# Reordering the first loads, casts and filler matmuls of a fused sigmoid-attention and MLP kernel on one core

## The chip, the core and the metric

The kernel runs on one core of a Trainium2 chip. The metric is device time in microseconds (us). Every run named here computed the right result. A profile is one execution; its span is some 1.8 us shorter than the time counted for that execution (388.1 against 389.91 us in the profile of before).

## The reference, cut to what matters

```python
# q, k, v: (8 batches, 12 heads, 448 rows, 64)
scores = scale * np.matmul(q, k.transpose(0, 1, 3, 2)) - np.log(S)
attn = 1.0 / (1.0 + np.exp(-scores))           # a sigmoid, no row sum
x = np.matmul(attn, v)                          # then reshaped to (3584, 768)
h = x @ w_in                                    # 768 -> 2048
g = 0.5 * h * (1.0 + np.tanh(c * (h + 0.044715 * h ** 3)))
out = g @ w_out                                 # 2048 -> 768
```

The kernel handles the heads in 24 groups of four. A group has seven column strips (`NJ`); one strip of one group is a unit: one score product on TensorE and one sigmoid of 128x896 values on ScalarE.

## The kernel before: the parts that the change touches

The kernel contains a planner. It plays the program forward with assumed costs and fixes the order of the instructions of each engine and of each queue. These orders are written into the program, so constants in the planner (assumed costs) act only through the order that they lead to.

k and q of group 0 arrive in two parts each, so that the first transposes can begin early. The later groups come in one transfer each.

```python
CUTS = ((0, NJ // 2 + 1), (NJ // 2 + 1, NJ))        # strips 0-3 and 4-6, for k and q
...
if g == 0:
    for x, (lo, hi) in enumerate(CUTS):
        # SyncE's queue: k.0, one half of q.1, k.1.   ScalarE's queue: q.0, the other half of q.1
        both = [plan.add(Op("ld%s0.%d.%d" % (nm, x, c), eng, ...))
                for (eng, c, w) in ((("SP", 0, 1), ("AQ", 1, 1)) if (nm, x) == ("q", 1) else
                                    (("AQ" if nm == "q" else "SP", 0, 2),))]
...
ld[g] = plan.add(Op("ld%s%d" % (nm, g), "AQ" if (nm, g) == ("q", 1) else "SP", ...))
...
who = "ACT" if (nm, x) == ("q", 0) else "DVE"       # which engine casts a part of group 0
```

Here k.0 is the first part of k, q.1 the second part of q, and k1 and q1 are k and q of group 1. `SP` is SyncE's queue, `AQ` ScalarE's, `DVE` is VectorE. A part that has landed is cast to bf16 (`qb`, `kb` in the profile), transposed on TensorE into `ps`, the program's PSUM tensor, and copied from there to `qT` or `kT`, which the score products read (a copy of 384 columns took 0.36 us on VectorE in the kernel before); then the scores of unit 0 can start.

Until there is real work, TensorE gets dummy matmuls. They are meant to have its clock granted in full by then. In the profile of before a matmul of 128 columns takes 107 ns at 5.1 us and 56 ns at 7.7 us; the turn is between 6.5 and 6.6 us, 5.0 us after the first dummy.

```python
def fn(e):
    return mm(ps[:, bank, 0:256], ident[:], gT[:, 0, 0:256], start=True, stop=True)
op = Op("warm", "PE", fn, [eye, blank, bank_free[bank]], 113.0 if plan.now > 6000.0 else 218.0, 165.0, mode=128)
...
if op is None and t < WARM and eye.end is not None and eye.end <= t and free_pairs(t) >= 2 and (...):
    return make_warm()
```

One helper does all casts and copies, so in the profile they share a line: L355 on VectorE and L354 on ScalarE, told apart by their tiles. The other lines are L412 dummies, L557 transposes of groups 0 and 1, L603 scores, L614 sigmoids of the first 21 units, L651 value products, L738 and L783 the two products of the MLP. In the changed kernel they are three to four lines further down, L358 and L357, L416, L560, L606, L617, L654, L741 and L786; some experiments move them a little more.

## Time and profile before

| | before |
|---|---|
| time, median of 3 runs (lowest to highest) | 390.36 us (390.03 to 390.97) |
| span of the profiled execution | 388.1 us |
| first sigmoid starts | 7.47 us |
| hole before the fifth sigmoid | 0.41 us |
| sixteenth sigmoid ends, and TensorE takes over as the bound | 21.06 us |

The page's busy times and two of its groups of instructions follow. In a group the columns are: line, engine, operation, output and input tiles, shapes, count, then busy time and mean ns of one, then the idle time of the engine just before them and what ended it.

```profile
PE 380.9 (98%) x3189; PEld 202.4 (52%) x3189; DVE 154.6 (40%) x268; ACT 228.2 (59%) x342; POOL 49.6 (13%) x82
...
L614 ACT ACTIVATE at<-ps 128x896 bf16<-128x896 f32 x21 | 17.2, 934 | 1.1 <-PE ps L603 1.1
...
L412 PE MATMUL ps<-gT,ident 128*128 128x256 bf16 x25 | 5.5, 380 | 1.5 <-POOL ident L362 1.5
```

TensorE is busy for 98% of the span, so there is little to win and it must be in the first 21 us. The 21 sigmoids of L614 were waited for 1.1 us in all: 0.66 before the first and 0.41 in the hole before the fifth. The dummies begin at 1.5 us, when GpSimd has made the identity.

### The profile page before, as it was taken

How to read it: one execution, taken by the hardware profiler on the slowest of the kernel's cores; microseconds unless marked ns; L12 is line 12 of the kernel's file. 1: busy time of each engine (PE TensorE's matmuls, PEld its weight loads, DVE VectorE, ACT ScalarE, POOL GpSimd, SP SyncE). 2: the span in 40 equal slices, each digit the busy share in tenths (PEclk: the TensorE clock that was granted, in tenths of full speed). 3: DMA queues.
4: the chain of work that ended last, by engine and by line, in shares of the span. 5: the costliest groups of instructions: out<-in, count | busy, mean ns of one | idle time of the engine just before them, and what ended most of it. 6: DMA issues, size and time to landing. Idle time of an engine off the chain costs nothing.

```text
span 388.1 us, 7458 instructions
## 1 busy us (share of the span) xinstructions
PE 380.9 (98%) x3189; PEld 202.4 (52%) x3189; DVE 154.6 (40%) x268; ACT 228.2 (59%) x342; POOL 49.6 (13%) x82
## 2 busy tenths in 40 slices
PE   7899999999999999999999999999999999999996
PEld 5434445545555555555555555555555555555565
DVE  3446633137760276404782068533571541000000
ACT  5999963258764575547684487655674772333221
POOL 5993110001200111001120011101000000000000
PEclk9999999999999999999999999999999999999999
DMA  8999999627791299804899247864472101111133
GB/s 228 195 203 203 210 207 311 138 64 183 188 225 26 59 208 196 200 2 120 184 243 197 47 109 175 219 121 95 113 195 53 42 2 41 43 41 42 41 83 81
DMA packets 64209, 51.74 MB, mean 133 GB/s; under 512 B 36272, under 2 KB 60720, under 8 KB 64176
## 3 DMA queue, kind: packets, MB, share of 16 engines
q1 hardware_dynamic: 48880, 36.77, 37.5%
q0 software_dynamic: 14528, 13.64, 23.1%
q10 hardware_dynamic: 768, 0.86, 0.7%
q8 instruction: 25, 0.41, 0.4%
q14 instruction: 8, 0.07, 0.0%
HBM read 45.61 MB, written 11.01 MB: 146 GB/s over the span
## 4 chain that ended last, share of the span: by engine, by line
PE 94%; ACT 3%; DMA 2%; DVE 0%; ACTq 0%; issue 0%
PE ps L783 38%; PE ps L738 37%; PE ps L603 9%; PE ps L651 8%; ACT at L614 3%; DMA qf<-in_q_dram 2%; PE ps L714 1%; PE ps L560 1%; ACTq L465 0%; DVE qb L355 0%; DVE kb L355 0%; PE ps L557 0%; ACT ob L354 0%
## 5 line engine op out<-in xcount | busy, mean ns | idle before, releaser
L623 ACT ACTIVATE th<-ps 128x896 f32<-128x896 f32 x147 | 127.5, 932 | 52.1 <-PE ps L603 52.1
L783 PE MATMUL ps<-w_out,gT 128*128 128x384 bf16 (+2 forms) x912 | 153.4, 323 | 0.0
L738 PE MATMUL ps<-xT,w_in 128*128 128x448 bf16 x750 | 148.0, 353 | 0.0
L783 PEld LDWEIGHTS ps<-w_out,gT 128*128 128x128 bf16 x912 | 86.9, 98 | 63.4 <-ACT th L623 3.7
L738 PEld LDWEIGHTS ps<-xT,w_in 128*128 128x128 bf16 x750 | 71.4, 98 | 71.9 <-issue 5.6
L627 DVE TENSOR_SCALAR at<-th 128x896 bf16<-128x896 f32 x147 | 91.7, 630 | 40.0 <-ACT th L623 39.0
L752 ACT ACTIVATE gT<-ps 128x448 bf16<-128x448 f32 x128 | 69.5, 554 | 63.7 <-PE ps L738 63.4
L355 DVE COPY ob<-ps 128x384 f32<-128x384 f32 x39 | 21.6, 554 | 75.1 <-PE ps L783 74.8
L603 PE MATMUL ps<-qT,kT 64*64 64x448 bf16 x672 | 48.1, 358 | 2.1 <-ACT at L614 1.7
L489 POOL DMA_DIRECT2D vb<-in_v_dram x24 | 15.0, 623 | 231.4 <-PE ps L603 228.3
L651 PE MATMUL ps<-at,vb 64*64 64x448 bf16 x672 | 38.2, 350 | 0.0
L603 PEld LDWEIGHTS ps<-qT,kT 64*64 64x64 bf16 x672 | 15.5, 105 | 26.5 <-issue 12.8
L354 ACT ACTIVATE ob<-ps 128x384 f32<-128x384 f32 (+2 forms) x18 | 8.5, 472 | 34.2 <-PE ps L783 34.2
L651 PEld LDWEIGHTS ps<-at,vb 64*64 64x64 bf16 x672 | 19.5, 107 | 12.2 <-issue 0.7
L355 DVE CAST kb<-kf 128x896 bf16<-128x896 f32 (+2 forms) x21 | 12.7, 606 | 27.6 <-DMA kf<-in_k_dram 27.6
L355 DVE CAST xT<-ps 128x448 bf16<-128x448 f32 x26 | 15.9, 622 | 11.1 <-PE ps L651 11.1
L614 ACT ACTIVATE at<-ps 128x896 bf16<-128x896 f32 x21 | 17.2, 934 | 1.1 <-PE ps L603 1.1
L355 DVE CAST qb<-qf 128x896 bf16<-128x896 f32 (+1 forms) x20 | 12.4, 618 | 10.7 <-DMA qf<-in_q_dram 10.5
L491 POOL DMA_DIRECT2D vb<-in_v_dram x24 | 15.8, 659 | 0.1
L354 ACT ACTIVATE xT<-ps 128x448 bf16<-128x448 f32 x22 | 12.2, 559 | 1.9 <-PE ps L651 1.9
L840 POOL DMA_DIRECT2D w_in<-in_moe_w_in_dram x16 | 9.9, 656 | 0.0
L412 PE MATMUL ps<-gT,ident 128*128 128x256 bf16 x25 | 5.5, 380 | 1.5 <-POOL ident L362 1.5
(30 smaller groups left out, 43.9 us busy)
## 6 DMA issues: line engine op xcount, KB each, us to landing
out_dram<-ob SPq DMA_DIRECT2D x54, 192.0 KB, 2.8
kf<-in_k_dram SPq DMA_DIRECT2D x19, 448.0 KB, 5.4
qf<-in_q_dram SPq DMA_DIRECT2D x18, 448.0 KB, 6.3
vb<-in_v_dram POOLq DMA_DIRECT2D x48, 112.0 KB, 5.7
w_in<-in_moe_w_in_dram POOLq DMA_DIRECT2D x16, 192.0 KB, 10.7
w_out<-in_moe_w_out_dram POOLq DMA_DIRECT2D x4, 768.0 KB, 21.9
kb<-in_k_dram POOLq DMA_DIRECT2D x4, 224.0 KB, 8.5
qb<-in_q_dram POOLq DMA_DIRECT2D x4, 224.0 KB, 9.0
```

Of the source, the lines that this page charges most:

```text
L354: return e.activation(o, i, AF.Copy)
L355: return e.tensor_copy(o, i)
L489: a = plan.add(Op("ldv%da" % g, "SWQ", lambda e, d=dst[0:64], ap=lo: e.dma_start(d, ap), deps, 610.0, 0.0, prio=order_v(g), sem="ldv%da" % ...
L491: c = plan.add(Op("ldv%db" % g, "SWQ", lambda e, d=dst[64:128], ap=hi: e.dma_start(d, ap), deps, 610.0, 0.0, prio=order_v(g), sem="ldv%db" ...
L603: r = mm(ps[64 * half:64 * half + 64, (x, y)[a], 0:S], kv[d, a, j, :], qv[d, a, :, :], start=True, stop=True)
L614: lambda e: e.activation(at[as_][:], both, AF.Sigmoid, bias=bias, scale=scale),
L623: lambda e: e.activation(th[ts][:], both, AF.Tanh, bias=0.5 * bias, scale=0.5 * scale),
L627: lambda e: e.tensor_scalar(at[as_][:], th[ts][:], 0.5, 0.5, op0=ALU.mult, op1=ALU.add),
L651: r = mm(ps[64 * c:64 * c + 64, banks[a], 0:S], vb[s][d, slot, j, :], at[as_][d, a, :], start=(j == 0), stop=(j == NJ - 1))
L738: r = mm(ps[:, bank, 0:S], w_in[:, kt, fc * 128:(fc + 1) * 128], xT[xb][:, kt, :], start=(kt == 0), stop=(kt == KT - 1))
L752: lambda e: e.activation(gT[:, fc, col:col + S], ps[:, bank, 0:S], AF.Gelu_apprx_tanh),
L783: r = mm(ps[:, bank, 0:hi - lo], gT[:, fc, col:col + 128], w_out[:, fc, lo:hi], start=(fc == 0), stop=(fc == FC - 1))
```

## The change

The intent is to start the sigmoids earlier and to close the hole before the fifth. k is cut into strips 3+4, so its first part is smaller. SyncE's queue carries k.0, all of q.1, then k1 and q1; ScalarE's carries q.0, then k.1. VectorE casts and copies q.0 and ScalarE q.1, the other way round than before. The dummies need only a blank tile and are 128 columns wide near the first real work, and none is put just ahead of it (`coming`). k1 now comes before q1.

```diff
-    DMA_FIRST = {"SP": 0.0, "AQ": 0.0, "SWQ": 1300.0}
+    DMA_FIRST = {"SP": 500.0, "AQ": 700.0, "SWQ": 1300.0}
...
+            w = 256 if plan.now < FINE else 128
-                return mm(ps[:, bank, 0:256], ident[:], gT[:, 0, 0:256], start=True, stop=True)
+                return mm(ps[:, bank, 0:w], gT[:, 0, 0:128], gT[:, 0, 0:w], start=True, stop=True)
...
-        CUTS = ((0, NJ // 2 + 1), (NJ // 2 + 1, NJ))
+        CUTS = {"q": ((0, NJ // 2 + 1), (NJ // 2 + 1, NJ)), "k": ((0, 3), (3, NJ))}
...
-                                for (eng, c, w) in ((("SP", 0, 1), ("AQ", 1, 1)) if (nm, x) == ("q", 1) else
-                                                    (("AQ" if nm == "q" else "SP", 0, 2),))]
+                                for (eng, c, w) in (("AQ" if (nm, x) in (("q", 0), ("k", 1)) else "SP", 0, 2),)]
...
-                ld[g] = plan.add(Op("ld%s%d" % (nm, g), "AQ" if (nm, g) == ("q", 1) else "SP",
+                ld[g] = plan.add(Op("ld%s%d" % (nm, g), "SP",
...
-                        who = "ACT" if (nm, x) == ("q", 0) else "DVE"
+                        who = "ACT" if (nm, x) == ("q", 1) else "DVE"
...
+        def coming(t):
+            wait = [cast.get(g if x is None else (g, x)) for (g, nm, src, dst, cast, tr, freed, after, x) in trans[:1]]
+            ends = [d.end for d in wait if d is not None]
+            ...
+            return any(e is not None and t < e <= t + NEAR for e in ends)
...
-            if op is None and t < WARM and eye.end is not None and eye.end <= t and free_pairs(t) >= 2 and (
+            if op is None and t < WARM and blank.end is not None and blank.end <= t and not coming(t) and free_pairs(t) >= 2 and (
```

The remaining lines of the diff are assumed costs. Only the first groups' instructions change their order; everything later stands in the same order on every engine.

More of the change, by code (lines that the diff above doesn't have):

```diff
@@ L319, in bass_sigmoid_attention__then__act_gelu_tanh_kernel @@
     WARM = 11000.0
+    FINE = 3400.0
+    FIRST = 44.0
+    NEAR = 50.0
     HOLD = 200.0
@@ L409, in make_warm @@
             bank = take(plan.now)
+            w = 256 if plan.now < FINE else 128
             def fn(e):
-                return mm(ps[:, bank, 0:256], ident[:], gT[:, 0, 0:256], start=True, stop=True)
-            op = Op("warm", "PE", fn, [eye, blank, bank_free[bank]], 113.0 if plan.now > 6000.0 else 218.0, 165.0, mode=128)
+                return mm(ps[:, bank, 0:w], gT[:, 0, 0:128], gT[:, 0, 0:w], start=True, stop=True)
+            op = Op("warm", "PE", fn, [blank, bank_free[bank]], w * (0.44 if plan.now > 6500.0 else 0.84), 165.0, mode=128)
             give(bank, op)
@@ L462, in load_qk @@
                 if g == 0:
-                    for x, (lo, hi) in enumerate(CUTS):
+                    for x, (lo, hi) in enumerate(CUTS[nm]):
                         both = [plan.add(Op("ld%s0.%d.%d" % (nm, x, c), eng,
@@ L467, in load_qk @@
                                             [], 490.0, 0.0, prio=(2, -3 if x == 0 else -2 if nm == "q" else -1),
-                                            sem="ld%s0.%d.%d" % (nm, x, c), pkt=(8 * w, 89.0 * (hi - lo) / NJ)))
-                                for (eng, c, w) in ((("SP", 0, 1), ("AQ", 1, 1)) if (nm, x) == ("q", 1) else
-                                                    (("AQ" if nm == "q" else "SP", 0, 2),))]
+                                            sem="ld%s0.%d.%d" % (nm, x, c), pkt=(8 * w, FIRST * (hi - lo) / NJ)))
+                                for (eng, c, w) in (("AQ" if (nm, x) in (("q", 0), ("k", 1)) else "SP", 0, 2),)]
                         ld[(0, x)] = All(both)
@@ L504, in cast_qk @@
                 if g == 0:
-                    for x, (lo, hi) in enumerate(CUTS):
-                        who = "ACT" if (nm, x) == ("q", 0) else "DVE"
+                    for x, (lo, hi) in enumerate(CUTS[nm]):
+                        who = "ACT" if (nm, x) == ("q", 1) else "DVE"
                         cast[(0, x)] = plan.add(Op("cast%s0.%d" % (nm, x), who,
@@ L509, in cast_qk @@
                                                        e, o[:, :, lo:hi, :], i[:, :, lo:hi, :], w),
-                                                   [ld[(0, x)]] + ([lambda: tr_q.get((0, 1))] if (nm, x) == ("k", 1) else []), (hi - lo) * 100.0, (hi - lo) * 110.0 + 150.0,
+                                                   [ld[(0, x)]] + ([lambda: tr_q.get((0, 1))] if (nm, x) == ("k", 1) else []), (hi - lo) * (107.0 if who == "ACT" else 75.0) + 60.0, (hi - lo) * (107.0 if who == "ACT" else 68.0) + 190.0,
                                                    prio=(0, -9 if nm == "q" or x == 0 else -1)))
@@ L548, in make_trans @@
             to = ps[:, bank, 0:NJ * 64].bitcast(BF16)
-            lo, hi = (0, NJ) if x is None else CUTS[x]
+            lo, hi = (0, NJ) if x is None else CUTS[nm][x]
             low = low_load(nm, g)
@@ L566, in make_trans @@
             flat_o = dst[:].rearrange("p j x -> p (j x)")[:, 128 * lo:128 * hi]
-            if (nm, x) == ("q", 0):
+            if (nm, x) == ("q", 1):
                 alts = {"ACT": ((hi - lo) * 107.0 + 50, (hi - lo) * 107.0 + 190)}
             else:
-                alts = {"DVE": ((hi - lo) * 70.0 + 70, (hi - lo) * 70.0 + 190)}
+                alts = {"DVE": ((hi - lo) * 70.0 + 70, (hi - lo) * 68.0 + 160)}
             tr[key] = plan.add(Op("trc%s%s" % (nm, key), "ANY",
@@ L582, in qk_needs @@
                 return [tr_q.get(g), tr_k.get(g)]
-            return [tr_q.get((0, 0)), tr_q.get((0, 1)), tr_k.get((0, 0 if j < CUTS[0][1] else 1))]
+            return [tr_q.get((0, 0)), tr_q.get((0, 1)), tr_k.get((0, 0 if j < CUTS["k"][0][1] else 1))]
         def by_half(t):
@@ L1025, in enter @@
             return n < 2 * UB or state["last"] == "b" or not go_b or state["av"] < NG * min(B, state["a"][0] + 1)
+        def coming(t):
+            wait = [cast.get(g if x is None else (g, x)) for (g, nm, src, dst, cast, tr, freed, after, x) in trans[:1]]
+            ends = [d.end for d in wait if d is not None]
+            if state["n"] < len(units):
+                needs = qk_needs(*units[state["n"]])
+                if all(d is not None and d.end is not None for d in needs):
+                    ends.append(max(d.end for d in needs))
+            return any(e is not None and t < e <= t + NEAR for e in ends)
         def pe_busy(pl, t):
             op = pe_next(pl, t)
-            if op is None and t < WARM and eye.end is not None and eye.end <= t and free_pairs(t) >= 2 and (
+            if op is None and t < WARM and blank.end is not None and blank.end <= t and not coming(t) and free_pairs(t) >= 2 and (
                     not state["n"] or sum(1 for x in range(state["n"]) if tanh[x].end is None or tanh[x].end > t) >= 2):
```

## The prediction

> **What bounds the kernel now.** I read the page's chain of work first, then busy time by stretch, then the timeline of the first 12 us, then the idle time by releaser.
>
> ```profile
> PE 94%; ACT 3%; DMA 2%; DVE 0%; ACTq 0%; issue 0%
> ```
>
> The chain that ended last is matmul work for 94% of 388.1 us. ScalarE and a transfer hold the other 5%. The table by stretch (columns: stretch, its length, then busy us of PE, weight load, VectorE, ScalarE, GpSimd, then granted clock, DMA share, GB/s) says where these lie:
>
> ```profile
> 1.50:5.10 3.60, 3.58 (x17) 2.54 (x18) 0.43 (x1) 1.86 (x3) 0.46 (x1) 1.00 0.86 274
> ...
> 7.04:11.20 4.16, 3.17 (x36) 1.47 (x37) 2.34 (x5) 3.34 (x4) 4.16 (x8) 1.00 1.19 189
> ...
> 19.00:21.10 2.10, 1.48 (x24) 0.37 (x16) 0.99 (x2) 2.10 (x4) 2.10 (x4) 1.00 1.24 201
> ...
> 61.00:200.00 139.00, 139.00 (x1132) 73.64 (x1130) 68.37 (x119) 81.79 (x118) 12.01 (x18) 1.00 0.65 150
> ```
>
> From 21.1 us TensorE is busy in every stretch without a hole, until the last matmul at 385. Before that it has holes, and ScalarE is full. So the kernel has three stages: a head until the first sigmoid, a sigmoid stage in which ScalarE paces everything, and a TensorE stage of fixed length. The diff touches only the head and the first group or two. Its whole worth is how much earlier the TensorE stage can begin, and that is how much earlier the sixteenth sigmoid ends (21.06 us). The chain in order of time names that stretch:
>
> ```profile
> 1.80 7.09 DMA qf<-in_q_dram
> 8.89 0.02 issue
> 8.91 0.73 DVE qb L355
> 9.64 0.60 DVE kb L355
> 10.25 0.05 issue
> 10.29 0.56 PE ps L557 x7
> 10.86 0.34 PE ps L603 x4
> 11.20 0.02 issue
> 11.22 9.84 ACT at L614 x12
> ```
>
> Columns are start, length, what. The binding thing is not the first sigmoid but the load of q for group 1: it lands at 8.89, VectorE casts q, then k; TensorE transposes k, and only behind those transposes stands the score product of unit 4 (a unit is one score tile pair and its sigmoid). ScalarE had run four sigmoids from 7.47 and then had nothing:
>
> ```profile
> 7.47 3.34 ACT L614 ACTIVATE at<-ps 128x896 bf16<-128x896 f32 x4 [0.66 <-PE ps L603]
> 11.22 2.54 ACT L614 ACTIVATE at<-ps 128x896 bf16<-128x896 f32 x3 [0.41 <-PE ps L603]
> ```
>
> The 0.41 in brackets is the hole. The starts within these runs are 0.80 to 0.82 us apart, the pace of ScalarE. So two terms can be won: the hole, and an earlier first sigmoid. They add, because all later sigmoids follow at the same pace.
>
> The head itself:
>
> ```profile
> 4.73 0.63 ACT L354 ACTIVATE qb<-qf 128x512 bf16<-128x512 f32 x1 [0.95 <-DMA qf<-in_q_dram]
> 5.12 0.63 PE L557 MATMUL ps<-ident,kb 128*128 128x128 bf16 x4
> 5.34 0.36 DVE L355 CAST qb<-qf 128x384 bf16<-128x384 f32 x1 [0.55 <-DMA qf<-in_q_dram]
> 5.54 0.95 PE L557 MATMUL ps<-ident,qb 128*128 128x128 bf16 x7
> 6.54 0.36 DVE L355 COPY qT<-ps 128x384 bf16<-128x384 bf16 x1 [0.32 <-PE ps L557]
> 7.04 0.57 PE L603 MATMUL ps<-qT,kT 64*64 64x448 bf16 x8
> ```
>
> The second part of q lands at 5.24 (the cast waits for it), is cast by 5.70, but its three transposes start only at 5.97: eleven stand in a row at 107 ns each, begun at 5.12 though k's cast was done at 4.79, because dummies (213 ns each) were still in front. Copy to 6.89, scores at 7.04, sigmoid at 7.47. Landing to sigmoid: 2.23 us.
>
> [...]both queues together reach 343 to 388 GB/s between 3.5 and 7 us[...]. [...]between 5 and 6 us I count 281 KB on ScalarE's queue against 51 on SyncE's. So who stands beside q's second part matters. [...]The trace shows 107 ns per 128-column transpose at 5.1 to 6.2 us and 56 ns at 7.7 us, the turn near 6.5, 5.0 us after the first dummy at 1.52.
>
> **The change part by part.**
>
> Transfers. Per DMA engine a descriptor takes 36 ns at 768 bytes (3 strips), 46 at 1024 (4), 74 at 1792 (all 7) in this trace, 16 of them per engine for a two-half transfer. Before, q's second part is complete after 16x46 (k's first) + 16x46 (q's first) + 2x8x36 = 2.05 us of engine time. After, if nothing else is served: 16x36 + 16x46 + 16x36 = 1.89 us, which is 0.16 earlier, landing 5.1. But k's second part now shares ScalarE's queue and can take turns with it[...]. I take 5.2, an estimate between them. k's first part gets smaller and should land 0.1 to 0.4 earlier than 4.34.
>
> Engines. ScalarE now casts and copies q's second part, 384 columns. From its rows for 512 columns (629 and 597 ns) and 0.85 ns a column, an estimate from the sigmoid's 934 ns at 896, the cast is 0.52 and the copy 0.49; VectorE took 0.36 for either. That costs 0.29. What it buys: k has three transposes instead of four, the dummies are 128 columns wide (107 ns) near the casts, and TensorE is kept free just ahead of a transpose, so q's last three need not queue. Sum from landing: 0.02 + 0.52 cast + 0.07 hand-over + 0.53 transposes (2x0.107 + 0.314, cold) + 0.04 + 0.49 copy + 0.08 + 0.43 scores to sigmoid = 2.18 us, so first sigmoid at 7.38 against 7.47: 0.09 won. VectorE's four-strip part (landing about 4.5, cast 0.43, four transposes, copy 0.42) ends about 6.0 and hides.
>
> Dummies. They no longer wait for the identity (1.52) but only for the blank tile (about 1.05). They are beside everything; they may bring the warm clock 0.45 earlier[...]. A warm clock would make the transposes 0.2 shorter.
>
> Group 1. k goes before q on SyncE's queue, both behind 384 KB. So k lands about 8, is cast and transposed by 9.5 at the latest, and unit 4 is needed at 7.38 + 4x0.81 = 10.62. The hole of 0.41 goes. Now q lands last, near 9.4 (same total bytes as before, when the last landed at 9.33). In the new TensorE order its transposes stand before unit 5: 9.4 + 0.75 cast + 0.06 + 0.39 + 0.19 (one value product) + 0.43 = 11.22 for unit 5's sigmoid, needed at 7.38 + 5x0.81 = 11.43. It hides, with 0.2 to spare. The instruction order of the other engines is unchanged after the first three groups.
>
> Sum: 0.41 + 0.09 = 0.50 us off 390.36, so 389.86; I say **389.85**. Weights follow: the first w_in slice landed at 22.77 and is used at 24.1, so half a microsecond fits.
>
> **The rivals.** First, q of group 1 becomes the wait: if it lands at 9.8, unit 5 starts at 11.62, against 12.04 before, and the gain is held to 0.4 whatever the head does: 389.95. For it: 0.2 of slack, GpSimd's loads start earlier since they wait for k's first part and take turns with q. Against: the total bytes are the same. Second, the second half of q lands at 5.4 behind k's second part and ScalarE's slower two steps stay: first sigmoid 7.6, the hole still gone, gain 0.3: 390.1. Third, the warm clock comes early and q lands at 5.1: first sigmoid 7.1, gain 0.75 (then the first rival caps it): 389.6. Fourth, the gap left ahead of the transposes delays the warm clock past 8 us: unit 0 and 1 at half pace, loss of 0.2 to 0.4: no gain at all.
>
> **Range and chances.** The rivals span 389.5 to 390.4. The three runs of before span 0.94 us, so the median carries some 0.3 of its own. Range 389.2 to 390.4. Two per cent is 7.8 us, and the whole head is 7.47, so faster than that is not to be had; nothing on the TensorE stage gets longer. Faster 0.01, within 2% 0.98, slower 0.01.
>
> **What would show each step.** First sigmoid at 7.1 to 7.6, q's second part landing at 5.1 to 5.4, ScalarE's cast 0.52 and copy 0.49. No idle before ScalarE's fifth sigmoid; sixteenth ending about 20.55; TensorE without a hole afterwards, last matmul about 384.5. The prediction is wrong if a hole opens before the sixth sigmoid (first rival), if TensorE waits for w_in near 23.5, or if the first sigmoid is earlier than 7.0 (transfers then served the small parts better than I worked out).

The forecast's sum is 0.41 + 0.09 = 0.50 us off 390.36, which gives 389.86 and was put as 389.85. Of the terms behind the 0.09, the working of the late end of q.1's landing, 5.4 us, is cut; the 5.2 used is the author's estimate between 5.1, worked out from the descriptor times of the trace of before (36 ns for 768 bytes, 46 for 1024), and that 5.4. The 0.45 us for an earlier full clock was an estimate too, from the starts of the dummies at 1.52 and about 1.05, and is not in the sum; measured, the matmuls turn to full pace between 6.5 and 6.6 us in both profiles (6.56 and 6.52 us in the record of the clock), though the dummies of the kernel after begin 0.43 us earlier.

## The result and the profile after

| | before | after |
|---|---|---|
| time, median (lowest to highest, runs) | 390.46 us (390.03 to 390.97, 4) | 389.75 us (389.67 to 390.08, 4) |
| span of the profiled execution | 388.1 us | 388.0 us |
| k.0 and q.0 landed | 4.34, 4.71 us | 4.21, 4.59 us |
| q.1 landed | 5.24 us | 5.45 us |
| k.1 landed | 7.19 us | 5.88 us |
| k1 and q1 landed | 9.33, 8.89 us | 7.16, 8.93 us |
| first sigmoid | 7.47 us | 7.57 us |
| hole before the fifth sigmoid | 0.41 us | none |
| sixteenth sigmoid ends | 21.06 us | 20.64 us |

The ratio of the two kernels is 0.9983 (95% interval 0.9966 to 1.0). Here and below a ratio is the mean time of one kernel's runs over the mean of the other's in the same rounds, so it is not quite the ratio of the quoted medians. The profiled executions took 389.91 and 389.75 us, so the two profiles have only 0.16 us between them to explain, less than the 0.7 us between the medians.

The page after, first the shares of the chain of work that ended last, then the sigmoids' and the dummies' groups:

```profile
PE 92%; ACT 4%; DMA 3%; issue 0%; DVE 0%; SPq 0%
...
L617 ACT ACTIVATE at<-ps 128x896 bf16<-128x896 f32 x21 | 17.1, 941 | 0.5 <-PE ps L606 0.5
...
L416 PE MATMUL ps<-gT 128*128 128x128 bf16 (+1 forms) x30 | 4.9, 329 | 1.6 <-DVE gT L408 1.1
```

The sigmoids' wait fell from 1.1 to 0.5 us, and 0.49 of that is the wait before the first. The dummies now begin after 1.1 us instead of 1.5, and there are 30 instead of 25. The transfers' share of the chain rose from 2% to 3%, which the last part of this section takes up.

The chain in order of time, from the load of q.1 on (start, length, what):

```profile
1.26 4.19 DMA qf<-in_q_dram
...
5.47 0.53 ACT qb L357
...
6.05 0.52 PE ps L560 x3
...
6.59 0.50 ACT qT L357
...
7.13 0.41 PE ps L606 x4
...
7.57 13.08 ACT at L617 x16
```

The chain now enters the sigmoid stage through the head, not through q1: q.1 lands at 5.45, is cast by ScalarE in 0.52 us, transposed, copied in 0.49 us, and sixteen sigmoids follow without a break. Group 1 stands in the timeline (start, busy time, engine, line, operation) like this:

```profile
8.98 0.63 DVE L358 CAST qb<-qf 128x896 bf16<-128x896 f32 x1
...
9.66 0.56 PE L560 MATMUL ps<-ident,kb 128*128 128x128 bf16 x7
...
10.16 0.38 PE L606 MATMUL ps<-qT,kT 64*64 64x448 bf16 x4
```

q1 is cast as soon as it has landed, and the score product of unit 4 begins at 10.16 us, before its sigmoid's turn. So the hole is closed.

Now the later stage. The kernel after is 0.41 us ahead at the sixteenth sigmoid, yet ends only 0.14 us ahead (its last matmul starts at 384.62 us, against 384.76). The chains show where the difference went. Before:

```profile
260.75 2.39 PE ps L738 x12
...
272.54 0.50 PE ps L603 x8
273.04 1.32 PE ps L651 x28
274.37 0.38 PE ps L603 x8
274.74 2.38 PE ps L738 x12
```

After:

```profile
260.34 2.39 PE ps L741 x12
...
267.11 5.94 DMA kf<-in_k_dram
...
273.08 0.06 DVE kb L358
...
273.62 0.56 DVE ob L358
...
274.23 0.38 PE ps L606 x4
274.61 2.38 PE ps L741 x12
```

At 260 us the lead is still 0.41 us (260.75 against 260.34). At 274.6 it is 0.13 us. In between TensorE waited for VectorE, as the timeline of the kernel after has it (the brackets hold the idle time and what ended it):

```profile
273.08 0.63 DVE L358 CAST kb<-kf 128x896 bf16<-128x896 f32 x1 [4.19 <-DMA kf<-in_k_dram]
...
273.62 0.55 DVE L358 COPY ob<-ps 128x384 f32<-128x384 f32 x1
...
274.23 0.11 PEld L606 LDWEIGHTS ps<-qT,kT 64*64 64x64 bf16 x4 [0.51 <-DVE ob L358]
```

VectorE stood still for 4.19 us in front of a cast whose load (k of group 22) had not landed. Behind that cast stood the copy of an output tile, which frees the PSUM banks that the next score product needs. That load took 5.94 us here and 5.61 in the profile of before, where the same cast ended early enough to leave no hole. So a stage that had no hole in one execution has one in another, and the orders of the instructions there are the same in both kernels.

### The profile page after: what moved, and what is told of

Its sections match the earlier page's. It is cut to its first block, busy times and chain, and to the rows that moved or that the text cites. A ratio compares the mean times of both kernels' runs of the same rounds, so it can differ in the third digit from the quotient of the medians.

```text
span 388.0 us, 7466 instructions
## 1 busy us (share of the span) xinstructions
PE 380.8 (98%) x3194; PEld 202.1 (52%) x3194; DVE 154.3 (40%) x268; ACT 228.1 (59%) x342; POOL 50.4 (13%) x82
## 4 chain that ended last, share of the span: by engine, by line
PE 92%; ACT 4%; DMA 3%; issue 0%; DVE 0%; SPq 0%
PE ps L786 38%; PE ps L741 37%; PE ps L606 9%; PE ps L654 7%; ACT at L617 3%; DMA kf<-in_k_dram 2%; DMA qf<-in_q_dram 1%; PE ps L717 1%; PE ps L563 1%; DVE ob L358 0%; ACT qb L357 0%; PE ps L560 0%; ACT qT L357 0%; SPq L469 0%; ACT ob L357 0%
## 5 line engine op out<-in xcount | busy, mean ns | idle before, releaser
L358 DVE CAST qb<-qf 128x896 bf16<-128x896 f32 (+1 forms) x20 | 12.3, 613 | 7.3 <-DMA qf<-in_q_dram 7.2
L416 PE MATMUL ps<-gT 128*128 128x128 bf16 (+1 forms) x30 | 4.9, 329 | 1.6 <-DVE gT L408 1.1
```

The source lines that it names most:

```text
L358: return e.tensor_copy(o, i)
```

## The experiments

Twelve runs were made, in four sets, each on one chip: the first four below; then the late casts, the swap and q1 on ScalarE's queue; then the nine dummies and the kernel before again; then the best version. The kernel before ran in the rounds of the first, third and fourth set. The second set, on the chip of the first, is held against the eleven runs of before of the first set and one more. "Hole" means idle time of ScalarE between two sigmoids, or of TensorE after 21 us. Landing times are those of the completion in the trace.

### The change again

No edit. The question is how large the effect is beside the spread between runs.

> The changed kernel unaltered, for its spread and a second profile. Every theory: ratio to the kernel before 0.998, as in the result (389.75 against 390.46 us). In the profile: first sigmoid near 7.57, sixteenth ending near 20.64. Open: whether the TensorE hole of 0.43 us at 273.8 us, seen in one profile, comes back (my theory: yes, within 0.2, because VectorE stands in front of a k load that takes 5.6 to 6 us).

Median 390.27 us (389.66 to 392.06, 6 runs), the kernel before 390.08 (389.46 to 390.94, 11 runs); ratio 1.0007 (0.9989 to 1.0026). The gain of the first measurement is not there. The head of this profile behaves like the first one's: first sigmoid 7.64, no hole, sixteenth ending at 20.71. But the late wait grew:

```profile
274.60 0.11 PEld L606 LDWEIGHTS ps<-qT,kT 64*64 64x64 bf16 x4 [0.81 <-DVE ob L358]
```

It is the same place as before, with 0.81 in place of 0.51, which is more than the 0.2 us that I had allowed. Two things therefore needed an explanation: this late hole, and the single run of 392.06 us.

### Only the order of group 1, on the kernel before

```diff
-ld[g] = plan.add(Op("ld%s%d" % (nm, g), "AQ" if (nm, g) == ("q", 1) else "SP",
+ld[g] = plan.add(Op("ld%s%d" % (nm, g), "SP",
```

q1 goes behind k1 on SyncE's queue. If the order k1, q1 is what closes the hole, this alone should close it. The edit does more than that, though: the planner answered it with another order on the engines. VectorE casts k1 first, and on TensorE the transposes of k1 and q1 each stand one unit earlier, those of q1 now in front of the fifth score product and not behind it.

> The kernel before with one edit: q of group 1 goes behind k of group 1 on SyncE's queue. Theory A (the gain is the hole before the fifth sigmoid, which the load of q for group 1 made): the hole of 0.41 us goes, first sigmoid stays at 7.47, sixteenth ends at 20.6, and the kernel is as fast as or 0.1 us faster than the changed one, ratio 0.998 to 0.9985. Theory B (the gain comes from the head: new strips, short dummies, earlier warm clock): no gain, ratio 0.9995 to 1.0005, and a hole stays.

The expectation missed. Median 391.15 us (390.88 to 391.35, 5 runs) against 390.08; ratio 1.0023 (1.0008 to 1.0038), so it is slower by 0.2%. The first sigmoid comes at 7.34, but:

```profile
9.59 0.38 PE L603 MATMUL ps<-qT,kT 64*64 64x448 bf16 x4
...
10.14 0.66 DVE L355 CAST qb<-qf 128x896 bf16<-128x896 f32 x1 [1.11 <-DMA qf<-in_q_dram]
...
10.85 0.56 PE L557 MATMUL ps<-ident,qb 128*128 128x128 bf16 x7 [0.89 <-DVE qb L355]
...
11.35 0.38 PE L603 MATMUL ps<-qT,kT 64*64 64x448 bf16 x4
...
11.79 1.73 ACT L614 ACTIVATE at<-ps 128x896 bf16<-128x896 f32 x2 [0.85 <-PE ps L603]
```

k1 landed at 8.38 and q1, issued at 2.74, only at 10.12. VectorE waited for it 1.11 us and ScalarE lost 0.85 us before the fifth sigmoid, whose score product (11.35) stands behind q1's transposes (10.85). This is the wait of the prediction's first rival, one unit earlier because of the moved order. With the order of before the same landing would still leave a hole of some 0.4 us before the sixth sigmoid (an estimate: the scores of 11.35 led to a sigmoid at 11.79, and the sixth is due at 7.34 + 5 x 0.81 = 11.39). The run is a loss, but how much of it is the loads' order and how much TensorE's is not separated; and of the 1.38 us by which its profile is longer than that of before, only 0.55 stand at the sixteenth sigmoid (21.61 against 21.06), the rest was lost later. In the full change something else must bring q1 in earlier.

### The change with k.1 on SyncE's queue

```diff
-for (eng, c, w) in (("AQ" if (nm, x) in (("q", 0), ("k", 1)) else "SP", 0, 2),)
+for (eng, c, w) in (("AQ" if (nm, x) == ("q", 0) else "SP", 0, 2),)
```

This takes k.1 away from the side of q.1. Between 4 and 5 us the kernel after moved 213 packets on SyncE's queue, where q.1 stands, and 212 on ScalarE's, where k.1 stands. If k.1 beside it is what delayed q.1 to 5.45, then q.1 should land earlier.

> The changed kernel with k's second part of group 0 moved from ScalarE's queue to SyncE's, behind q's second part; nothing else moves. Theory A (q's second part landed at 5.45 and not 5.1 because k's second part took turns with it on the other queue): it lands at 5.0 to 5.15, first sigmoid 7.2 to 7.3, sixteenth ends near 20.3, 0.3 us less than the changed kernel, unless a wait later takes it back. Rival: landing is set by the start of SyncE's queue or by its smaller descriptors, stays at 5.4, and nothing moves.

Half of it held. The engines' orders are those of the kernel after. q.1 landed at 5.22 and the first sigmoid came at 7.17, 0.40 earlier than in the kernel after. But q1, now issued fifth on the queue at 2.78, landed at 10.15:

```profile
12.22 0.92 ACT L617 ACTIVATE at<-ps 128x896 bf16<-128x896 f32 x1 [0.89 <-PE ps L606]
```

The hole of 0.89 us, before the sixth sigmoid, is the prediction's first rival as it was written. It took more than the head gave; the sixteenth sigmoid ended at 21.24. Median 390.81 us (389.62 to 392.04, 6 runs), ratio 1.0016 (0.9997 to 1.0034). Together with the run before it, this shows what the parts are for. k.1 on ScalarE's queue costs some 0.2 us of q.1's landing (5.45 against 5.22, one profile each), and it brings q1 from 10.15 to 8.93. Without it the new order of group 1 leaves a hole in both profiles. Why one more entry on SyncE's queue costs q1 over 1 us, when it is issued only 0.5 us later and the bytes are the same, was not settled. The traces show that q1's last packets come slowly beside GpSimd's loads between 8 and 10 us (21 packets of SyncE's queue in this run, 28 in the run before, 1 in the kernel after); that the packets of GpSimd's queue hold them up is argued, not shown.

### The change with one late cast moved

```diff
+    + ([lambda: ev_o.get((16, 0))] if (nm, g) == ("k", 22) else [])      # an added dependence of the cast
```

The cast of k for group 22 goes behind the copy of the output tile that stood behind it. If the copy behind the waiting cast makes the hole at 274 us, it goes.

> The changed kernel with one swap on VectorE, at 273 us: the copy of output strip 16's first half goes before the cast of k for group 22, which waits for its load. Theory A (the 0.27 us that the changed kernel loses between 273 and 280 us in its profile is the copy waiting behind that cast, and with it a PSUM bank): no TensorE hole over 0.33 us after 21 us, and 0.2 to 0.3 us less than the changed kernel, ratio near 0.9975. Rival (a fault of that one profile, or the delay moves to the next wait): same time as the changed kernel within 0.1 us.

The hole at 274 us is gone, and the median is 389.90 us (389.43 to 390.58, 6 runs), ratio 0.9993 (0.9979 to 1.0006). But the profiled execution, the longest of the six, has the same thing at another place:

```profile
202.35 0.63 DVE L358 CAST kb<-kf 128x896 bf16<-128x896 f32 x1 [1.90 <-DMA kf<-in_k_dram]
...
206.71 1.50 PE L742 MATMUL ps<-xT,w_in 128*128 128x448 bf16 x7 [0.83 <-DVE ob L358]
```

A cast waited 1.90 us for its load, VectorE ran late, and some 4 us further on TensorE waited for an output copy. So there are several such places, and which of them opens differs from one execution to the next.

### Four late casts moved, on both kernels

```diff
+    + ([lambda: ev_o.get((0, 0))] if (nm, g) == ("q", 6) else [])
+    + ([lambda: ev_o.get((16, 0))] if (nm, g) == ("k", 22) else [])
+    + ([lambda: ev_o.get((12, 0))] if (nm, g) == ("k", 17) else [])
+    + ([lambda: ev_o.get((12, 0))] if (nm, g) == ("q", 17) else [])
```

The same four dependences were added to the kernel before and to the changed one. With the late holes out of the way, the difference between the two should be the head's.

> The kernel before, with four casts on VectorE moved behind output copies so that no cast that waits for a load stands ahead of a copy that frees a PSUM bank (q of group 6 behind the first copy of strip 0, k and q of group 17 behind that of strip 12, k of group 22 behind that of strip 16). Theory C (the spread of all kernels, 389.4 to 392.1 us, is made by TensorE holes at 65, 206 and 274 us, whose length is that of a load's flight): no hole over 0.33 us after 22 us, spread of five runs below 0.5 us, median 0.1 to 0.5 us below the kernel before (its own profile had no such hole, its runs of 390.6 to 391 would). Rival D (the spread comes from elsewhere): spread and median as before.

> The changed kernel with the same four casts moved. Theories A and C: the head's 0.35 to 0.45 us, lost or hidden in the holes until now, shows in the time: 0.4 us below f1_before_late, about 389.4 us, spread below 0.5 us. Rival: the gain of the head is taken back wherever TensorE meets a transfer that does not come earlier with it; then f2_after_late equals f1_before_late within 0.1 us.

Before with late casts: median 389.76 us (389.61 to 390.3), ratio 0.9993 (0.9979 to 1.0007). After with late casts: median 389.60 us (389.44 to 391.89), ratio 0.9996 (0.9976 to 1.0016). So a version of before with a calmer later stage reaches the time of the change, though neither ratio is clear of 1. The medians differ by 0.16 us where 0.4 was expected, and neither spread stayed below 0.5 us: it is 0.7 for before, and the after version has one run of 391.89. Its profile has no late hole; that of before has one left, 0.38 us at 289 us, a place that the four moves don't touch.

The profile of the before version held a surprise in the head, where nothing was edited:

```profile
7.65 4.96 ACT L618 ACTIVATE at<-ps 128x896 bf16<-128x896 f32 x6 [0.78 <-PE ps L607]
```

The run of sigmoids goes through the fifth without a hole. q1 landed at 7.97 here, not at 8.89, and k1 at 8.77. The sixteenth sigmoid ended at 20.72. So the hole of 0.41 us that the whole prediction rests on was the size of one execution.

### q's parts swapped back between the engines

```diff
-who = "ACT" if (nm, x) == ("q", 1) else "DVE"
+who = "ACT" if (nm, x) == ("q", 0) else "DVE"
```

On top of the change with late casts, ScalarE takes q.0 and VectorE q.1, as before. VectorE is faster at it (0.36 against 0.52 us for a cast of three strips), so the head should gain. The planner moved dummies too: three instead of two stand behind k's transposes and four instead of six behind q's last.

> As f2_after_late, and ScalarE takes q's first part of group 0 and VectorE its second, as in the kernel before (the queues and strips stay those of the change). The term of my sum under test: ScalarE's slower cast and copy cost 0.29 us on the last leg, so with q landing at 5.45 to 5.7 the first sigmoid comes at 7.3 (7.2 to 7.4) and not at 7.51 to 7.64; sixteenth ending 20.35 to 20.45; 0.2 us below f2_after_late. Rival: TensorE's transposes or the clock set the first sigmoid and it stays at 7.5.

The expectation missed, and not by a little: median 391.61 us (389.45 to 392.06, 6 runs), ratio 1.0027 (1.0006 to 1.0048). Five of six runs lie at 390.87 or above. The table by stretch of the profiled execution (stretch, length, busy us of PE, weight load, VectorE, ScalarE and GpSimd, granted clock, share of the transfer engines, GB/s) says why:

```profile
4.10:7.50 3.40, 1.98 (x29) 1.24 (x26) 1.77 (x5) 1.23 (x2) 2.95 (x5) 1.00 1.08 377
7.50:14.40 6.90, 6.38 (x61) 3.10 (x57) 2.91 (x6) 4.94 (x6) 6.90 (x12) 0.51 1.26 203
14.40:21.00 6.60, 5.54 (x108) 2.50 (x100) 2.40 (x4) 6.60 (x9) 6.60 (x11) 1.00 1.25 202
```

The granted clock is 1.00 from 4.1 to 7.5 us, then half for 6.9 us, then full again. In the half stretch ScalarE waits at every second or third sigmoid:

```profile
7.68 1.73 ACT L621 ACTIVATE at<-ps 128x896 bf16<-128x896 f32 x2 [1.30 <-PE ps L610]
9.88 1.76 ACT L621 ACTIVATE at<-ps 128x896 bf16<-128x896 f32 x2 [0.48 <-PE ps L610]
12.11 0.92 ACT L621 ACTIVATE at<-ps 128x896 bf16<-128x896 f32 x1 [0.46 <-PE ps L610]
13.86 9.93 ACT L621 ACTIVATE at<-ps 128x896 bf16<-128x896 f32 x12 [0.84 <-PE ps L610]
```

The sixteenth sigmoid ends at 22.98 us instead of 20.70, which is the 2 us that the run is too long. In the stretch ahead of the loss TensorE was busy 1.98 of 3.40 us, in pieces: its longest gap there is 0.62 us. So the full clock was taken back after a stretch that was 58% busy; what took it back the trace doesn't show.

The change keeps TensorE free just ahead of a transpose and makes its dummies short. When the clock is granted early, as here at 4.1 us, the same dummies also take half the time (56 instead of 107 ns for 128 columns) and leave more of the stretch empty. That is the conjecture for the long runs, and not yet a test of it. The share of busy time alone doesn't decide it either: the unaltered change of the first experiment also got its clock early, at 4.0 us, and kept it with the same share of work (1.96 of 3.40 us) and with a longer gap (0.71 us).

```profile
4.10:7.50 3.40, 1.96 (x30) 1.23 (x28) 1.81 (x5) 1.01 (x2) 2.91 (x5) 1.00 1.08 373
```

### The change with q1 on ScalarE's queue

```diff
-ld[g] = plan.add(Op("ld%s%d" % (nm, g), "SP",
+ld[g] = plan.add(Op("ld%s%d" % (nm, g), "AQ" if (nm, g) == ("q", 1) else "SP",
```

> The changed kernel with q of group 1 back on ScalarE's queue, behind k's second part; the order on the computing engines is unchanged. Theory A (the hole before the fifth sigmoid goes because k of group 1 lands early, alone on the queues, and not for the new strips or dummies): q of group 1 now takes turns with k of group 1, k lands at 8.5 to 9.3 and not 7.1 to 7.2, and a hole of 0.1 to 0.4 us comes back before the fifth or sixth sigmoid. Theory B (strips and dummies did it): no hole, sixteenth ends near 20.64.

Median 390.39 us (389.66 to 392.62, 6 runs), ratio 1.0011 (0.9988 to 1.0035). For its own question it is inconclusive. k1 landed at 8.08 and q1 at 8.98, but the profile fell into an execution at half clock, so the sigmoids tell nothing of the loads. (In the kernel after, the casts of k1 and q1 began at 8.45 and 8.98, so these landings alone give no reason for a hole; that there is none at full clock isn't shown.)

```profile
6.48 0.85 PE L416 MATMUL ps<-gT 128*128 128x128 bf16 x6
...
10.87 0.93 PE L560 MATMUL ps<-ident,kb 128*128 128x128 bf16 x7
...
13.48 0.37 PE L606 MATMUL ps<-qT,kT 64*64 64x448 bf16 x4
```

Seven transposes take 0.93 us here and 0.56 in the kernel after. The clock column nevertheless shows 1.00 for this run, and its page has no row of the clock; here the pace of a known instruction has to be read instead. The run does show that the unswapped change can fall into the half clock as well (the sixteenth sigmoid ended at 22.93), with two of its six runs above 392 us. But it is not the loss of the run before. There the clock was granted and taken back; here it came late. A matmul of 128 columns takes 107 ns from the last of the first dummies, at 3.4 us, to the transposes of q1 at 12.3, and the wider dummies before that 213 ns; the first matmuls at full pace stand at about 13.2 us. This is the prediction's fourth rival, only far longer than the "past 8 us" of its text.

### Nine dummies added, with q swapped and unswapped

```diff
+PADS = {"trpk(0, 0)": 3, "trpq(0, 1)": 4, "qk0.0": 2}
...
 op = pe_next(pl, t)
+if op is not None and op.name in PADS:
+    extra = [make_warm(0.0) for _ in range(PADS.pop(op.name))]
+    state["queue"] = extra[1:] + [op] + state["queue"]
+    return extra[0]
```

Three 128-column dummies are put ahead of k's first transposes, four between q's two parts and two ahead of the first scores; no other instruction moves. That the gaps on TensorE cost the clock, whether it is taken back or granted late, is conjecture (theory E below): in the swapped version TensorE stood empty for 1.42 of the 3.40 us from 4.1 to 7.5 us, and the clock then fell to half (seven transposes took 0.93 us there, 0.56 in the kernel after). If it is right, the long runs disappear in both versions. If it was the swap, they stay in the swapped one.

> As f3_after_late_swap, with nine more 128-column dummies on TensorE: three ahead of k's first transposes, four between q's first and second part, two ahead of the first scores; no other order changes. Theory E (f3 ran at 390.9 to 392.1 in five of six runs [...]the full clock, already granted, was taken back for 6.8 us, and every transpose and score took twice as long): no run above 390.6, the clock full without a break from 4 to 8 us on, first sigmoid at 7.2 to 7.4, 389.2 to 389.6 us. Rival: the slow runs come from the swap on ScalarE and VectorE (order of casts), and stay.

> As f2_after_late, with the same nine dummies. Theory E: no run near 392 (f2 had one of six, the changed kernel one of ten), five runs within 0.6 us, median 389.5 us, as f2. Rival (the runs near 392 are of another kind, any kernel has them now and then): one in six or so stays.

Swapped: median 389.76 us (389.68 to 389.83, 5 runs), ratio 0.9994 (0.9981 to 1.0006), where five of six runs had been long, on another chip. The stretches of its profile:

```profile
4.10:7.50 3.40, 3.15 (x34) 2.53 (x36) 1.78 (x5) 1.23 (x2) 2.89 (x5) 1.00 1.08 376
7.50:14.40 6.90, 5.87 (x85) 2.52 (x80) 3.02 (x7) 6.61 (x9) 6.90 (x12) 1.00 1.27 206
```

TensorE is busy 3.15 of 3.40 us. But this is not the case that was lost, with the dummies filled in: in this execution the clock was granted only at 6.6 us (the matmuls of 128 columns take 107 ns until then and 56 after; the column reads 1.00 for the slow part too), so the added dummies ran at the slow pace. From then on the clock stays. The first sigmoid missed what I had expected and came at 7.79 us; the median is 0.2 us above the expected range.

Unswapped: median 389.49 us (389.43 to 389.96, 5 runs) against 389.97 (389.58 to 390.72, 9 runs) for before; ratio 0.9990 (0.9978 to 1.0003). First sigmoid 7.45, sixteenth ending at 20.55, no late hole; the clock came at 5.5 us. So no profile with the nine dummies had the clock as early as 4.1 us, and that they keep it in that case rests on the counts of runs alone.

The counts over all runs point that way. The kernels that have the change's dummies as they are had 40 runs, and 8 of them took 391.8 us or more. One of the eight (392.04, with k.1 on SyncE's queue) ran at full clock and is explained by its holes. The kernels with the old dummies had 50 runs, none above 391.35. The kernels with nine more had 15, none above 389.96. For the swapped version, with five of six runs long before and none of five after, that is plain. Without the swap, four of 34 runs were long at half clock, or may have been, and none of the ten with nine more dummies; that can be chance. Only two of the long runs at half clock were profiled in that state, the swapped version's, where the clock was taken back, and that of q1 on ScalarE's queue, where it came late. Two more, 392.06 us of the swapped version and 392.62 us of q1 on ScalarE's queue, have a mean granted clock of 0.991, which is what 6.9 us at half clock make of a span of 390 us (1 - 0.5 x 6.9 / 390). The long runs of the unaltered change (392.06), of the late casts (391.89) and one more of the swapped version (391.91) have records of 1.0 and 0.999. So has the profiled run in which the clock came late (392.09, 1.0), and they may be of that kind; none of them was profiled, and it isn't shown.

### The kernel before again

No edit, with a profile of its own, in the same set as the nine dummies.

> The kernel before unaltered, for a second profile of its head. Theory A (the hole of 0.41 us before the fifth sigmoid is built into its order of loads): hole of 0.2 to 0.6 us, first sigmoid 7.4 to 7.7. Theory F (the hole was one execution's: in f1_before_late, whose head is the same, q and k of group 1 landed at 7.97 and 8.77, 0.6 to 0.9 us earlier, and there was none): a hole under 0.1 us in this profile, or one of another size with the loads landing otherwise; sixteenth sigmoid ending at 20.6 to 20.8 where there is none. Time as before, 390.1 us, no run above 391.

Median 390.79 us (389.8 to 390.95, 5 runs), ratio 1.0009 (0.9995 to 1.0023) to its own twin, so a median of five runs can be 0.8 us off. The head:

```profile
10.88 1.73 ACT L614 ACTIVATE at<-ps 128x896 bf16<-128x896 f32 x2 [0.23 <-PE ps L603]
```

This time the hole is 0.23 us, with the first sigmoid at 7.30, q1 landed at 8.53 and the sixteenth sigmoid ending at 20.71. With the other two profiles of this head the hole measures 0.41, 0.23 and 0.00 us. The execution took 390.92 us because of two late holes, in which matmuls of TensorE started 0.96 us apart at 273.9 and 0.75 at 290.1 us.

### The best version again

No further edit: the change with four late casts moved and nine dummies added, on another chip.

> h2_after_dummies once more, for its interval: head of the change, nine more dummies, four casts behind output copies. If the three causes found so far are all (loads of the head, holes behind late casts, clock taken back): five runs between 389.3 and 390.0 us, none near 392, no TensorE hole over 0.33 us after 22 us, ratio to the kernel before 0.998 to 0.9995. Rival: h2's 389.49 was luck of a few runs; then the median is 390 and a slow run or a late hole comes.

Median 389.42 us (389.34 to 389.66, 5 runs) against 390.49 (389.68 to 390.99, 9 runs); ratio 0.9971 (0.9957 to 0.9984). In this set it is faster than before by 0.3% (in the third set by 0.1%, not clear of 1). Two expectations missed: the ratio lies below the expected 0.998 to 0.9995, and a late hole, 0.41 us between matmuls at 289 us, was there. The chain has the sixteen sigmoids without a break:

```profile
7.48 13.11 ACT at L621 x16
```

Over its two sets this version's ten runs lie between 389.34 and 389.96 us, the eighteen of before in the same rounds between 389.58 and 390.99. It was not run in the same rounds as the unaltered change, so against that one there is no ratio.

## Why the prediction was right, and where its reasons failed

**The number.** 389.85 us was predicted and 389.75 measured, inside the range. Part of that is luck. The runs of one kernel differ by 1 us and more, and the second set gave 390.27 for the change against 390.08 for before. Taking both sets, the ten runs of the change have a median of 390.0 us, the sixteen of before 390.2. The call "within 2%" was safe, for the reason given: the head is too short for more.

**The three stages and what paces them: right.** In all profiles with full clock the sigmoids follow at 0.8 us from the first to the sixteenth, apart from the holes described, and TensorE takes over after the sixteenth. What is won by then arrives at 260 us undiminished (0.41 in the two first profiles).

**"The hole of 0.41 goes": right, but mis-sized.** It was gone in every profile of the changed head at full clock that kept k.1 on ScalarE's queue. But 0.41 was the size in one execution; the three profiles of the old head have 0.41, 0.23 and none, following the landing of q1 at 8.89, 8.53 and 7.97 us. The sixteenth sigmoid ended at 21.06, 20.71 and 20.72 us in these, and at 20.64, 20.71, 20.58 and 20.70 us in the four of the changed head at full clock (the change twice, and with one and with four late casts moved). The means are 20.83 and 20.66, so the head is worth about 0.2 us, not 0.50. That is an estimate from three and four profiles, and it hangs on the one with 21.06: the other two of the old head ended as early as the new.

**"0.09 won" before the first sigmoid: wrong, even in sign.** It came at 7.57 us and not 7.38. The step that failed is the landing of q's second part: 5.2 was taken, between 5.1 and 5.4, and 5.45 measured (5.69 in the second profile). The second rival had it: k.1 stands beside q.1 on the other queue. Moving k.1 away brought the landing to 5.22 and the first sigmoid to 7.17. The later terms of that sum held: cast 0.52, copy 0.49, and 2.12 us from landing to sigmoid against 2.18 worked out. Two readings on the way were loose without harm: 934 ns at 896 columns and 629 at 512 make 0.79 ns a column, not 0.85; and the view of 5 to 6 us has 0.28 MB on ScalarE's queue against 0.07 on SyncE's, not 51 KB: an uneven share, and no more than that.

**Group 1.** "k lands about 8" and "q near 9.4" were too late by 0.8 and 0.5 us (7.16 and 8.93), so it hides with more to spare than was said. That margin hangs on k.1 standing on ScalarE's queue. I had counted this part of the change only as a cost. Without it q1 lands at 10.15, and the first rival comes true with a hole of 0.89 us.

**"From 21.1 us TensorE is busy in every stretch without a hole": true of that one profile, wrong as a rule.** This is the step that I had not questioned. In the kernel after some 0.27 of the 0.41 us was lost at 274 us, to a cast on VectorE that waited for its load in front of a copy that frees PSUM. The order of the casts and copies is the same in both kernels; the loads' time differs between executions. Moving one cast closed that place, and moving four closed all but one at 289 us. These holes, more than the head, seem to make the run-to-run spread at full clock: the profiled executions of before took 389.91 us without such a hole and 390.92 us with two.

**The fourth rival, a gap that harms the clock: the loss of clock is real, in its own form and in one I had not thought of; that the gap makes it is not shown beyond the counts of runs.** I expected the full clock to come late and to cost 0.2 to 0.4 us. In one of the two long runs that were profiled it did come late, at about 13.2 us; in the other it came at 4.1, was taken back for 6.9 us and given again. Each cost about 2 us. With nine added dummies, and nothing else moved, no long run was seen, which is plain for the swapped version and may be chance for the other. The condition stays open: one execution kept its clock with the same share of busy time (1.96 of 3.40 us) with which another lost it (1.98), and the unaltered change got its full clock at 6.5 us in one profile and at 4.0 in the other.

**The third rival**, an early clock with an early q.1 and a sigmoid at 7.1, was not seen in the unaltered change. The early clock alone was, at 4.0 us in its second profile; the first sigmoid still came at 7.64, since q.1 landed at 5.69.

## What to carry to other kernels

A hole seen in one profile is one draw: read it in several executions before its length goes into a sum, and ask what sets its size, here the landing of a load. Don't put work that waits for a load in front of a copy that frees a buffer another engine needs: here VectorE stood 4.19 us before such a cast, and TensorE waited 0.51 us for the copy behind it. Fillers that are meant to keep a clock up should fill the real waits too: no run shows that keeping the engine free just ahead of the real work brought the first sigmoid forward (with nine dummies put in it came at 7.45 and 7.48 us, without at 7.51 to 7.64), and with the change's fillers as they were 8 of 40 runs took 391.8 us or more, with nine more none of 15 (two of the eight were profiled at half clock, and each had lost about 2 us). And an edit to a planner's input is one edit only if the order that comes out is compared; here one moved load moved transposes, and the fillers with them.
